# Filler matmuls in the waits of the first batch, another order of the first loads, later attentions, and loads held by semaphores, in a fused attention and FFN kernel

## Chip, cores, metric

One core of one Trainium2 chip. The metric is device time of the whole kernel in microseconds (us). The profile's span, from first to last instruction, is 1.7 to 3 us shorter than it, mostly 1.8. All runs here were of the fast state; ratios are the mean time of one kernel's fast runs over that of the other's of the same rounds, so not quite the ratio of the medians that are quoted beside them.

## The reference

Eight batches, 12 heads, 448 tokens, head size 64; then a gated FFN over all 3584 tokens.

```python
scores = np.matmul(q, k.transpose(0, 1, 3, 2)) / sqrt(64)
attn = np.maximum(scores, 0.0) ** 2 / 448
x = np.matmul(attn, v)            # (8, 12, 448, 64), then to (3584, 768)
g = x @ w_gate                    # 768 -> 1536
gelu = 0.5 * g * (1.0 + erf(g / sqrt(2)))
out = (gelu * (x @ w_val)) @ w_out
```

## The kernel before

The program is laid out ahead of time. Each piece of work is an `Op` with an assumed cost and with dependencies; `run_plan` goes through the queues in order of planned time and emits instructions in that order. The plan decides only the **order on each engine**; at run time semaphores alone hold anything. A dependency in the plan that isn't a data dependency holds nothing on the chip.

```python
# loads: queued on GpSimd, float32 in DRAM to bfloat16 in SBUF
def load(nbytes, emit, deps=(), cost=0.7):
    op = Op("POOL", cost, emit, deps)           # deps: for the plan only
    arrivals[op] = nbytes / 400e3
    POOL.append(op)
    return op
...
# order of the first loads
for h0, h1 in ((0, 2), (2, 4), (4, 8), (8, 12)):
    load_heads(0, h0, h1)                       # q, k, v of batch 0
load_w12(0)                                     # gate and value weights, 1 of 6
load_heads(1, 0, 4)
load_w12(1)
load_w12(2)
load_heads(1, 4, 8)
load_w12(3)
load_heads(1, 8, 12)
load_w12(4)
load_w12(5)
load_qk(2, 0, 0, H)
load_qk(2, 1, 0, H)
for i in range(FC // WOG):
    load_wo(i)                                  # output weights, 4 pieces
load_v(2, 0, H)
...
# q and k of batches 2 to 7 are turned by DMA: DVE copies into qkr, SyncE issues
copies = [Op("DVE", 0.4, lambda c=c: emit_copy(c), ...) for c in range(SC)]
tr_op[b] = [Op("SP", 1.1, lambda c=c: nc.sync.dma_start_transpose(...), ...) for c in range(SC)]
...
# where each batch's attention stands among the matmuls of the FFN
LEAD = 6.0
for b in range(B):
    if b == 0:
        lo, hi = -60.0, -12.0
    elif b == 1:
        lo, hi = -8.0, starts[1] - LEAD
    else:
        lo, hi = starts[b - 1] - LEAD, starts[b] - LEAD
```

In the profile PE is TensorE, ACT ScalarE, DVE VectorE, POOL GpSimd and SP SyncE (SPq: its DMA issues). `sp` are scores (PE), `rl` their ReLU (ACT), `attnT` its square (DVE), `ff` the PSUM tiles of everything else, `gel` the gelu (ACT), `uT` the gated product (DVE). TensorE is used as four 64x64 quarters.

## Time and profile before

| | before |
|---|---|
| time, median | 458.32 us (457.1 to 458.66) |
| span of the profiled run | 456.6 us |
| PE busy | 93% |
| mean granted clock | 0.950 |
| first gate matmul | 37.44 us |
| first gelu of batch 2 | 158.90 us |

The page, the windows, the waits and the chain are shown and read in the prediction. One line more, of the timeline of SyncE (start, length, what). It is the issue of batch 2's seven transposes:

```profile
61.85 26.17 SPq L248 DMA_TRANSPOSE qkT<-qkr  x7
```

### The profile page before, as it was taken

What the parts mean: (1) busy time and instruction counts of PE and PEld (TensorE: products, weight loads), DVE (VectorE), ACT (ScalarE), POOL (GpSimd) and SP (SyncE); (2) the same over time, 40 slices, a digit from 0 to 9 for tenths busy, and PEclk for the clock granted to TensorE, in tenths of its full rate; (3) what the DMA queues carried; (4) which work ended last, traced back from release to release, by engine and by line L of the source; (5) the groups of instructions that cost most, each with busy time, mean ns of one, the idle gap of its engine ahead of it and who ended that gap; (6) DMA issues with size and microseconds to landing.
All of it is one profiled execution on the core that took longest, in us unless ns stands there. A gap on an engine that the chain in (4) does not pass through costs nothing.

```text
span 456.6 us, 19815 instructions
## 1 busy us (share of the span) xinstructions
PE 423.8 (93%) x9192; PEld 366.7 (80%) x9192; DVE 206.0 (45%) x367; ACT 225.4 (49%) x322; POOL 70.7 (15%) x114
## 2 busy tenths in 40 slices
PE   5779997099999999999999999999999999999994
PEld 2546874078779987899999978899999878987894
DVE  1795574034574356634573357435653455212200
ACT  1786544035555655555555555555555655422221
POOL 9545421006000510033000600030000000000000
PEclk8597999579999999999999999999999999999997
DMA  7999999909455690749082873581272200120033
GB/s 99 191 198 198 201 199 168 191 3 182 83 79 82 109 190 7 121 87 200 15 118 60 141 143 38 88 137 41 15 112 73 72 3 3 37 72 3 3 83 93
DMA packets 75218, 44.92 MB, mean 98 GB/s; under 512 B 36224, under 2 KB 71552, under 8 KB 75136
## 3 DMA queue, kind: packets, MB, share of 16 engines
q0 software_dynamic: 37056, 24.39, 37.4%
q1 hardware_dynamic: 38080, 19.28, 22.2%
q8 instruction: 72, 1.18, 1.1%
q14 instruction: 10, 0.08, 0.0%
HBM read 48.76 MB, written 11.01 MB: 131 GB/s over the span
## 4 chain that ended last, share of the span: by engine, by line
PE 88%; DMA 3%; ACT 2%; POOL 2%; SPq 2%; DVE 2%; issue 1%; POOLq 0%; ACTq 0%; DVEq 0%
PE ff L151 79%; PE sp L151 8%; ACT rl L340 2%; SPq L248 2%; DMA qk<-in_k_dram 2%; DMA qkT<-qkr 1%; POOL qk L198 1%; POOL v L211 1%; PE ff L291 1%; DVE attnT L346 1%; DVE qkT L297 1%; DVE uT L438 0%; DVE xT L395 0%; ACT gel L433 0%; ACT osb L484 0%
## 5 line engine op out<-in xcount | busy, mean ns | idle before, releaser
L151 PE MATMUL ff<-xT,wv 64*64 64x448 bf16 x2304 | 223.4, 351 | 0.4 <-issue 0.4
L151 PE MATMUL ff<-xT,wg 64*64 64x448 bf16 x2304 | 222.4, 351 | 0.4 <-ACT gel L433 0.4
L340 ACT ACTIVATE rl<-sp 128x896 bf16<-128x896 f32 x168 | 152.4, 918 | 135.0 <-PE sp L151 105.4
L151 PE MATMUL ff<-wo,uT 64*64 64x384 bf16 x2688 | 151.1, 324 | 0.3 <-DVE uT L438 0.3
L151 PEld LDWEIGHTS <-wv 64*64 64x64 bf16 x2304 | 134.4, 107 | 15.7 <-issue 1.5
L151 PEld LDWEIGHTS <-wg 64*64 64x64 bf16 x2304 | 132.6, 107 | 15.9 <-issue 0.9
L346 DVE TENSOR_TENSOR attnT<-rl 128x896 bf16<-128x896 bf16 x168 | 104.0, 623 | 84.5 <-ACT rl L340 83.4
L151 PE MATMUL sp<-qkT 64*64 64x448 bf16 (+1 forms) x768 | 113.0, 349 | 20.6 <-DMA qkT<-qkr 14.2
L151 PEld LDWEIGHTS <-uT 64*64 64x64 bf16 x2688 | 127.1, 107 | 5.5 <-DVE uT L438 1.0
L438 DVE TENSOR_TENSOR uT<-gel,ff 128x448 bf16<-128x448 bf16 x96 | 59.5, 620 | 78.5 <-PE ff L151 75.6
L151 PE MATMUL ff<-attnT,v 64*64 64x448 bf16 (+1 forms) x768 | 91.5, 340 | 0.0
L433 ACT ACTIVATE gel<-ff 128x448 bf16<-128x448 f32 x96 | 52.1, 543 | 54.0 <-PE ff L151 51.6
L151 PEld LDWEIGHTS <-qkT 64*64 64x64 bf16 x768 | 47.7, 111 | 32.1 <-issue 26.2
L211 POOL DMA_DIRECT2D v<-in_v_dram x46 | 28.8, 651 | 197.4 <-PE ff L151 166.1
L151 PEld LDWEIGHTS <-v 64*64 64x64 bf16 x768 | 49.5, 111 | 3.5 <-issue 0.5
L395 DVE TENSOR_SCALAR xT<-ff 128x448 bf16<-128x448 f32 x48 | 29.9, 623 | 49.0 <-PE ff L151 46.8
L484 ACT COPY osb<-ff 128x384 f32<-128x384 f32 x56 | 26.7, 476 | 36.2 <-PE ff L151 36.2
L291 PEld LDWEIGHTS <-qk 64*64 64x64 bf16 x336 | 11.8, 136 | 7.8 <-DMA qk<-in_q_dram 3.1
L198 POOL DMA_DIRECT2D qk<-in_k_dram x23 | 14.7, 641 | 15.6 <-DMA wo<-in_moe_w_out_dram 8.6
L291 PE MATMUL ff<-ident,qk 64*64 64x64 bf16 x336 | 13.0, 221 | 4.2 <-DMA qk<-in_q_dram 2.9
L198 POOL DMA_DIRECT2D qk<-in_q_dram x23 | 14.9, 673 | 9.9 <-PE ff L151 6.3
L240 DVE COPY qkr<-qk 128x768 bf16<-128x768 bf16 x42 | 13.4, 356 | 0.0
(17 smaller groups left out, 30.2 us busy)
## 6 DMA issues: line engine op xcount, KB each, us to landing
out_dram<-osb SPq DMA_DIRECT2D x56, 192.0 KB, 2.7
v<-in_v_dram POOLq DMA_DIRECT2D x40, 128.0 KB, 5.6
qk<-in_q_dram POOLq DMA_DIRECT2D x20, 224.0 KB, 9.2
qk<-in_k_dram POOLq DMA_DIRECT2D x20, 224.0 KB, 9.8
wg<-in_moe_w_gate_dram POOLq DMA_DIRECT2D x6, 384.0 KB, 10.7
wv<-in_moe_w_val_dram POOLq DMA_DIRECT2D x6, 384.0 KB, 11.8
wo<-in_moe_w_out_dram POOLq DMA_DIRECT2D x4, 576.0 KB, 21.4
v<-in_v_dram POOLq DMA_DIRECT2D x2, 384.0 KB, 26.0
```

The source lines that it names most:

```text
L151: return nc.tensor.matmul(o, lhsT, rhs, start=start, stop=stop, tile_position=(P * row, P * col))
L198: op = load(4 * (h1 - h0) * S * D, lambda: nc.gpsimd.dma_start(tile_of().rearrange("p (h x) -> p h x", h=H)[:, h0:h1, :], src[b, h0:h1].re ...
L211: nc.gpsimd.dma_start(v16[b][HALF[i], h0:h1, :, :], v[b, h0:h1].rearrange("h (p c) d -> p h c d", c=SC)[:, :, c0:c0 + VC, :])
L240: nc.vector.tensor_copy(box[0][:, c], qk16[b].rearrange("p (h c d) -> p c h d", c=SC, d=D)[:, c])
L248: tr_op[b] = [Op("SP", 1.1, lambda c=c: nc.sync.dma_start_transpose(qkT_tile(b).rearrange("d (c r) x -> d c r x", c=SC)[:, c], box[0][:, c ...
L291: nc.tensor.transpose(t[HALF[j], pr, c * P:(c + 1) * P], src[HALF[i], 2 * (2 * m + pr) + j, c, :], ident[HALF[i], HALF[i]], tile_position= ...
L340: nc.scalar.activation(rl[:, :, :], box[0][:, :, 0:S], AF.Relu)
L346: nc.vector.tensor_tensor(a[:, :, :], box[1][:, :, :], box[1][:, :, :], op=ALU.mult)
L395: nc.vector.tensor_scalar_mul(xT[b][:, pr, :], box[0][:, 0:S], scalar1=out_scale)
L433: nc.scalar.activation(gel[b, fc][:, :], box[0][:, 0:S], AF.Gelu)
L438: nc.vector.tensor_tensor(uT[b][:, fc, :], gel.pop((b, fc))[:, :], box[0][:, 0:S], op=ALU.mult)
L484: nc.scalar.copy(ob[:, cols], box[0][:, 0:OGS])
```

## The change

Its intent: get PE through the start of the kernel sooner. (1) Where the plan leaves PE idle in the first 45 us, matmuls without a use are put in to keep its clock up. (2) The first loads come in larger pieces, weights before batch 1, output weights before q and k of batch 2. (3) Attention of batches 1 and 2 stands later among the FFN's matmuls. (4) Loads from batch 3 on get semaphores, so that what was only planned now holds; batch 3's are tied to later gates by three.

```diff
@@ run_plan: gaps of PE are offered to fill @@
         if e in together:
             floor = t
+            if t > busy:
+                fill(busy, t)
+            busy = max(busy, op.end)
@@ loads @@
     def load(nbytes, emit, deps=(), cost=0.7):
-        op = Op("POOL", cost, emit, deps)
+        def paced():
+            ins = emit()
+            for d in deps:
+                tc.add_manual_dep(ins.ins, d.ins.name, SYNC, reason="pace")
+
+        op = Op("POOL", cost, paced, deps)
@@ fillers (new; FILL = 45.0; new_bank also records the reader of each PSUM bank) @@
+    def fill(t0, t1):
+
+        n = int((t1 - t0 - 0.35) / 0.11)
+        if t1 > FILL or n < 2:
+            return
+        reader = in_bank[-FB] if len(in_bank) >= FB else None
+        if reader is not None and (reader.end is None or reader.end + 0.1 > t0):
+            return
+        t = new_bank(None)
+        for _ in range(n):
+            nc.tensor.matmul(t[:, 0:256], warm[:, 0:128], warm[:, 0:256], start=True, stop=True)
@@ add_gate_value: which gate releases which load @@
-            if b + 2 < B and b and fc < 9:
-                h0 = 4 * (fc % 3)
+            n = fc - (3 if b == 1 else 0)
+            if b + 2 < B and b and 0 <= n < 9:
+                h0 = 4 * (n % 3)
   ... (fc becomes n in the lines that follow)
@@ order of the first loads @@
-    for h0, h1 in ((0, 2), (2, 4), (4, 8), (8, 12)):
-        load_heads(0, h0, h1)
+    for h0, h1 in ((0, 4), (4, 8), (8, 12)):
+        load_qk(0, 0, h0, h1)
+        load_qk(0, 1, h0, h1)
+        if h0:
+            load_v(0, h0 - 4, h1 - 4)
+    load_v(0, 8, 12)
     load_w12(0)
+    load_w12(1)
     load_heads(1, 0, 4)
-    load_w12(1)
     load_w12(2)
+    load_w12(3)
     load_heads(1, 4, 8)
-    load_w12(3)
-    load_heads(1, 8, 12)
     load_w12(4)
     load_w12(5)
+    load_heads(1, 8, 12)
+    for i in range(FC // WOG):
+        load_wo(i)
     load_qk(2, 0, 0, H)
     load_qk(2, 1, 0, H)
-    for i in range(FC // WOG):
-        load_wo(i)
     load_v(2, 0, H)
@@ places of the attentions @@
-            lo, hi = -8.0, starts[1] - LEAD
+            lo, hi = 0.0, starts[1] - LEAD
+        elif b == 2:
+            lo, hi = starts[1] + 6.0, starts[2] - LEAD
```

Cut: the other uses of `new_bank`, `return` ahead of some `dma_start`, and the line that keeps the instruction of `uT` for the semaphore.

More of the change, by code (lines that the diff above doesn't have):

```diff
@@ L20, in __init__, with run_plan @@
         self.start = self.end = None
-def run_plan(queues, pools, arrivals, together):
+def run_plan(queues, pools, arrivals, together, fill):
     free = {e: 0.0 for e in (*queues, *pools)}
     at = {e: 0 for e in queues}
-    dma = last = floor = 0.0
+    dma = last = floor = busy = 0.0
     def ready(op):
@@ L119 @@
     FB = 4
+    FILL = 45.0
     EARLY = 2
@@ L178, in emit @@
         def emit(wt, src):
-            nc.gpsimd.dma_start(
+            return nc.gpsimd.dma_start(
                 wt[:, :, :], src[:, cols].rearrange("(c p) f -> p c f", p=128))
@@ L210, in emit @@
                 c0 = i * (SC - VC)
-                nc.gpsimd.dma_start(
+                return nc.gpsimd.dma_start(
                     v16[b][HALF[i], h0:h1, :, :],
@@ L258, with new_bank @@
     ring = [warm_op]
+    in_bank = []
+    def new_bank(reader, shape=(128, 512), dtype=f32):
+        in_bank.append(reader)
+        return psF.tile(list(shape), dtype, name="ff", tag="F")
+    def fill(t0, t1):
[8 more added lines that the diff above has]
+            nc.tensor.matmul(t[:, 0:256], warm[:, 0:128], warm[:, 0:256], start=True, stop=True)
     def ring_dep():
@@ L286, in emit @@
             if i not in box:
-                box[i] = psF.tile([128, 2, SC * P], bf16, name="ff", tag="F")
+                box[i] = new_bank(t_op[b, m, i], [128, 2, SC * P], bf16)
             t = box[i]
@@ L377, in emit @@
             if not box:
-                box[0] = psF.tile([128, 512], f32, name="ff", tag="F")
+                box[0] = new_bank(x_op[b, pr])
             if i == 1 and w == VC - 1:
@@ L422, in emit @@
             if not box:
-                box[0] = psF.tile([128, 512], f32, name="ff", tag="F")
+                box[0] = new_bank(done)
             if r == 1 and dc == 0:
@@ L437, in emit_mult @@
                 uT[b] = upool.tile([128, FC, S], bf16, name="uT", tag="uT")
-            nc.vector.tensor_tensor(uT[b][:, fc, :], gel.pop((b, fc))[:, :],
-                                    box[0][:, 0:S], op=ALU.mult)
+            u_op[b, fc].ins = nc.vector.tensor_tensor(
+                uT[b][:, fc, :], gel.pop((b, fc))[:, :], box[0][:, 0:S], op=ALU.mult).ins
         ops = [[Op(f"PE{r}", GS, lambda r=r, dc=dc: emit(r, dc),
@@ L450, in add_gate_value @@
             DVE.append(done)
-            if b + 2 < B and b and fc < 9:
-                h0 = 4 * (fc % 3)
-                if fc < 6:
-                    load_qk(b + 2, fc // 3, h0, h0 + 4, [done])
+            n = fc - (3 if b == 1 else 0)
+            if b + 2 < B and b and 0 <= n < 9:
+                h0 = 4 * (n % 3)
+                if n < 6:
+                    load_qk(b + 2, n // 3, h0, h0 + 4, [done])
                 else:
                     load_v(b + 2, h0, h0 + 4, [done])
-                if fc == 5:
+                if n == 5:
                     add_dma_transposes(b + 2)
@@ L469, in emit @@
             if not box:
-                box[0] = psF.tile([128, 512], f32, name="ff", tag="F")
+                box[0] = new_bank(cp)
             i, o = divmod(fc, WOG)
@@ L598, in emit_warm_up @@
     def emit_warm_up():
-        t = psF.tile([128, 512], f32, name="ff", tag="F")
+        t = new_bank(None)
         for _ in range(10):
@@ L606 @@
     run_plan({"PE0": PE0, "POOL": POOL}, {"PE1": PE1, "ACT": ACT, "DVE": DVE, "SP": SP, "IDLE": IDLE}, arrivals,
-             ("PE0", "PE1"))
+             ("PE0", "PE1"), fill)
 _INS = ['q', 'k', 'v', 'moe_w_gate', 'moe_w_val', 'moe_w_out']
```

## The prediction

> **What bounds the kernel now.** I read the page first, for the shape of the whole.
>
> ```profile
> PE   5779997099999999999999999999999999999994
> PEclk8597999579999999999999999999999999999997
> DMA  7999999909455690749082873581272200120033
> GB/s 99 191 198 198 201 199 168 191 3 182 83 79 82 109 190 7 121 87 200 15 118 60 141 143 38 88 137 41 15 112 73 72 3 3 37 72 3 3 83 93
> ```
>
> One slice is 11.4 us. From slice 10 on TensorE is full and at full clock: nothing to gain there but matmuls. The loss is in the first 100 us: clock at about half in slice 2, a hole in slice 8. DMA is flat at 191 to 201 GB/s from slice 2 to 6. Second view, the windows of that stretch (columns: length, then busy us of PE, weight loads, DVE, ACT, POOL, each with its count; clock, DMA share, GB/s).
>
> ```profile
> 0.00:10.00 10.00, 5.45 (x76) 2.84 (x76) 1.21 (x3) 1.28 (x1) 9.05 (x20) 0.90 0.73 89
> 10.00:20.00 10.00, 7.10 (x136) 4.38 (x140) 5.95 (x11) 7.12 (x9) 7.23 (x11) 0.50 1.32 185
> 20.00:30.00 10.00, 8.74 (x152) 6.01 (x154) 8.78 (x16) 8.91 (x12) 4.95 (x7) 0.75 1.41 198
> 30.00:40.00 10.00, 7.79 (x146) 5.17 (x141) 6.65 (x12) 6.20 (x8) 4.96 (x7) 0.76 1.41 198
> ...
> 80.00:90.00 10.00, 0.00 (x0) 0.00 (x0) 0.00 (x0) 0.00 (x0) 0.00 (x0) 0.50 1.26 191
> ```
>
> From 20 to 30 us ACT and DVE are near 90%: the first attention is bound by them, while PE is slow or waiting. From 80 to 90 us only DMA works. Third, the waits, and the chain through the hole (start, length, what).
>
> ```profile
> PE sp L151 <- DMA qkT<-qkr: 14.2, 1, 14.2
> ```
>
> ```profile
> 77.57 1.41 SPq L248
> 78.97 0.04 issue
> 79.02 6.17 SPq L248
> 85.22 6.42 DMA qkT<-qkr
> 91.64 0.14 issue
> 91.78 0.58 PE sp L151 x2
> ```
>
> The first scores of batch 2 (counted from 0) wait 14.2 us for its q and k, transposed by DMA. Fourth, the DMA view of two windows: batch 2's seven transposes (first line) against batch 3's (second).
>
> ```profile
> qkT<-qkr SPq DMA_TRANSPOSE x7, 13.5
> ```
>
> ```profile
> qkT<-qkr SPq DMA_TRANSPOSE x7, 2.8
> ```
>
> 13.5 us to landing against 2.8. The timeline of SyncE gives 26.17 us for issuing the first seven (from 61.85) and 10.32 for the others (from 128.88). In the first case batch 3's six q and k loads, issued by GpSimd between 61 and 75 us, share the engines.
>
> **What the Trainium skill says.** (1) "DMA: Bandwidth & Descriptors", section "Issuing engines are not separate DMA queues": transfers started by different engines run on the same 16 DMA engines and interleave. The 13.5 against 2.8 us agrees. (2) "TensorE: Matmul & The Clock Gate", Part 1: the array's clock is halved unless the recent window, some 3.4 us, was busy; an idle window brings it back to half. The trace agrees: 0.50 from 7 us, after a gap of 2.95, and 0.50 through the hole and until 97 us, 5 us after it. It also shows 0.50 between 35 and 43 us without a gap that long. (3) Same page, "Architectural detail": ACT and DVE take their instructions strictly in order, so one that waits for a load holds those behind it. The trace before doesn't show that decisively: its first copy into `qkr` starts at 61.25, and q and k landed at 61.0.
>
> **My ruler.** Four 64x64 matmuls of 448 columns share the array and cost 0.19 us (in the trace, successive pairs of the value matmuls start at 44.37, 44.56, 44.75, with gate pairs between). I walked through both compiled instruction orders and summed columns at that rate; "position" is that sum, in us of full-clock PE work. The whole is 396.4 before and 399.9 after. From the first gate of batch 2 (position 114.4, its gelu at 158.9 us) to PE's end at 450.9, 282.0 of position took 292.0 us: 1.035 us per unit of position. From that gate on the two orders of work are the same but for details, so I give the rest its measured length: 456.6 - 158.9 = **297.7 us**. What must be found is when the changed kernel reaches that gelu.
>
> **The change, part by part.**
>
> *Filler matmuls.* The order holds 32 more matmuls of 256 columns, in ten groups of 2 to 5, all before the first gate of batch 0: 3.4 us at full clock, in places where PE was planned to wait for ACT or DVE. Cost on the path 0 to 1 us. Their use is the clock: at half clock in the first attention 12 relus took 13.4 us (10.95 to 24.33), at full clock nine took 7.39. Worth 3 to 4 us of that stage, if they work.
>
> *Order of the first loads.* q and k of four heads first, v one group later; 18 issues become 12 for batch 0. GpSimd takes about 0.6 us per issue (1.21 us for two v of 64 KB), and before issued some 145 KB/us between 4 and 10 us, less than the 198 GB/s that DMA can do: so 89 GB/s in the first window. With larger pieces I expect full rate from about 4 us: 2.5 to 3 us earlier for everything behind.
>
> *Weights before batch 1, output weights before batch 2's q and k; second attention later.* The first gate (37.44 us before) had six score units of batch 1 before it, now one. Attention 0 starts near 8 instead of 10.95 and takes 18 to 21 us; q and k of batch 1's first heads land near 26; so the first gate is near 29.5, at position 19.6 (before: 17.0). But it isn't free to run from there. Landing times: bytes ahead over 0.1985 MB/us, plus an offset. Before, q, k of batch 2 had 10,176 KB up to and with them and landed at 61.0 (issue 45.30 + 15.7). Now they have the 2,304 KB of output weights ahead too: 12,480 KB, so 61.0 + 2.36 MB/0.205 (the rate at 50 to 60 us) = 72.5, less 2.5 to 3 for the earlier start: **69.5**.
>
> *A held DVE.* The first `qkr` copy of batch 2 stands in DVE's order before the last product into `uT` of batch 0. PE needs that one at position 56. PE itself gets there so: 29.5, plus 6.8 of position x 1.035 = 36.6 at batch 1's second transposes, whose q and k land near 38.2; then 29.6 x 1.035 = 30.6 to 68.9. The load is at 69.5 and four short DVE steps (2.3 us) follow: PE passes position 56 at **71.8**. So a wait of some 3 us, and a new bound: the loads.
>
> *Batch 3's loads held.* They now wait for DVE's products at positions from 74 on, some 91 us. Batch 2's transposes then share DMA only with v of batch 2 (0.79 MB, 4 us). Issue from 70.5 in some 10.3 us, plus 2 for sharing, plus 2.8: ready near 85.5. Their scores are at position 69.8 instead of 51.9: PE is there at 71.8 + 13.8 x 1.035 = 86.1. The 14.2 us wait and the 2.75 us lost to 5.5 us at half clock behind it go; I leave 1 us for a remainder.
>
> *Sum.* The gelu is at position 117.8: 71.8 + 61.8 x 1.035 + 1 = 136.8. Plus 297.7 = 434.5 of span. The time was 458.33 for the profiled run with 456.6 of span: add 1.7. **436 us**, 4.9% less.
>
> **The rivals.** (a) *The wait is replaced.* The hole was hidden DMA work; with 0.59 MB less of batch 3 in the way, but batch 2's q and k 11.5 us later in the queue, the transposes land late again, or PE stays half-clocked after the 3 us wait. For it: the queue is full until some 74 us in both orders. Against: scores moved by 17.9 of position. If 5 us of wait and 2.5 of cold clock remain: 443. (b) *Nothing of the start is gained*: DMA is bound by small pieces and not by GpSimd's issue rate, and filler does nothing. For it: 165 to 185 GB/s even at 10 to 16 us. Then q and k land at 72.5: 439. (c) *PE's own path is slower than I sum*, by cold clock in the first attention and fillers waiting for banks: gate 0 at 34 gives position 56 at 74: 438. (d) *Loads are faster* than my offset says: 69.5 becomes 67, PE's path binds: 433.
>
> **Range and chances.** The fixed 297.7 us is 65% of the time and hardly uncertain; all doubt lies in 136.8. The rivals cover 433 to 443; two together, or a stall I haven't seen, reach 446; all luck gives 429. Range 429 to 446. A result within 2% needs over 449.4, that is 13 us of new waits: 4%. Slower: 1%.
>
> **What would show it.** In the changed profile: first gate near 29.5 us; clock near full from 8 to 30; q and k of batch 2 landing near 69.5; a DVE wait of 0 to 4 us for them before a `qkr` copy, with PE idle some 3 us near 70; the seven transposes issued in 10 to 13 us; PE's wait for `qkT` under 3 us; batch 2's first gelu near 137; from there 298 us. The prediction is wrong if the wait for `qkT` is again above 6 us, if the clock falls to half for long after 30 us, or if the part behind that gelu isn't within 2 us of 297.7.

## The result, and the profile after

| | before | after |
|---|---|---|
| time, median | 458.32 us | 436.5 us (436.01 to 436.95) |
| ratio, 95% interval | | 0.9528 (0.9507 to 0.9549) |
| span of the profiled run | 456.6 us | 434.6 us |
| mean granted clock | 0.950 | 0.992 |
| first gate matmul | 37.44 us | 30.84 us |
| first gelu of batch 2 | 158.90 us | 137.60 us |
| from there to the end of the span | 297.7 us | 297.0 us |

21.3 of the 22.0 us of span were gained ahead of batch 2's first gelu. The page of the changed kernel, the rows that answer to those of before (slices of 10.9 us now):

```profile
PE   6999989999989999999999999999999999999995
PEclk9899999999999999999999999999999999999998
DMA  8999999826993679256933679357962100120034
GB/s 117 196 198 198 203 209 186 161 39 74 123 174 75 88 88 159 77 85 93 161 70 93 89 89 175 76 81 87 148 94 76 40 3 2 49 66 3 3 84 101
```

The hole is gone, and from slice 3 on the clock is at nine tenths or more. DMA still moves 196 to 209 GB/s from slice 2 to 6: the load queue is as full as before. The windows (same columns as in the prediction):

```profile
0.00:10.00 10.00, 6.48 (x89) 3.22 (x89) 2.15 (x4) 3.01 (x3) 7.51 (x17) 1.00 0.82 111
10.00:20.00 10.00, 9.14 (x208) 6.00 (x208) 7.66 (x14) 8.01 (x10) 7.21 (x10) 0.83 1.40 196
20.00:30.00 10.00, 9.16 (x171) 5.47 (x168) 9.21 (x18) 7.81 (x10) 4.93 (x7) 1.00 1.41 197
30.00:40.00 10.00, 9.83 (x205) 7.32 (x207) 5.38 (x10) 7.17 (x9) 4.50 (x6) 1.00 1.41 198
...
80.00:90.00 10.00, 10.00 (x215) 7.86 (x210) 2.65 (x5) 4.25 (x7) 0.00 (x0) 1.00 0.59 117
```

DMA moved 111 instead of 89 GB/s in the first 10 us: that's the new order and sizes, for every run with the old ones has 88 to 91 there, every run with the new ones 102 to 119. PE works through 80 to 90 us. The chain of the changed kernel through the place that had the hole:

```profile
51.04 19.61 DMA qk<-in_k_dram
...
70.73 0.36 DVE qkr L249
...
71.55 0.62 DVE qkr L249 x2
72.17 0.54 DVE uT L465
...
72.75 13.32 PE ff L155 x280
86.07 0.18 PE sp L155 x2
```

One reads it upwards: batch 2's scores at 86.07 follow 13 us of uninterrupted matmuls, those follow a product of DVE, that stands behind three copies into `qkr`, and those waited for k of batch 2, which landed 19.6 us after its issue. No wait stands between 72.75 and the scores: the last transpose had landed at 83.11.

This is one profile, though, and PE waited only 0.6 us for that product. In the profile of the same kernel run again (c_after, span 433.9 us) k landed at 70.77, and the chain passes the place on PE alone:

```profile
69.89 1.32 PE ff L155 x28
71.22 0.01 PE sp L155 x2
71.23 15.17 PE ff L155 x321
86.40 0.18 PE sp L155 x2
```

Here PE's own path and the load arrive within about a microsecond of each other. Of the six profiles that have holds, new places and new load order together (fillers in or out, batch 3's loads sooner or not), batch 2's load is in the chain of the first one only; the other five pass here by PE. The issue of the transposes, from SyncE's timeline of the changed kernel:

```profile
71.19 10.39 SPq L257 DMA_TRANSPOSE qkT<-qkr  x7
```

10.39 us instead of 26.17. The waits (total, times, longest, in us), those that matter of the first 110 us, and then PE's one wait for transposes in a wider window:

```profile
DVE qkr L249 <- DMA qk<-in_k_dram: 1.3, 1, 1.3
...
PE ff L155 <- DVE uT L465: 0.6, 1, 0.6
```

```profile
PE sp L155 <- DMA qkT<-qkr: 1.7, 1, 1.7
```

This 1.7 us isn't batch 2 but **batch 3**, whose last transposes landed at 126.28. Batch 3's loads, held three gates longer, made its own transposes late, which the prediction had not seen. (In c_after's profile they landed at 125.62, and PE stood 0.7 us at that place.)

### The profile page after: what moved, and what is told of

It reads as the page before. It is cut to its first block, busy times and chain, and to the rows that moved or that the text cites. A ratio compares the mean times of both kernels' runs of the same rounds, so it can differ in the third digit from the quotient of the medians.

```text
span 434.6 us, 19901 instructions
## 1 busy us (share of the span) xinstructions
PE 420.1 (97%) x9224; PEld 365.5 (84%) x9224; DVE 205.7 (47%) x367; ACT 225.5 (52%) x322; POOL 68.4 (16%) x110
## 3 DMA queue, kind: packets, MB, share of 16 engines
q0 software_dynamic: 36992, 24.39, 42.2%
HBM read 48.76 MB, written 11.01 MB: 138 GB/s over the span
## 4 chain that ended last, share of the span: by engine, by line
PE 86%; DMA 7%; ACT 2%; DVE 1%; issue 1%; POOL 1%; POOLq 0%; ACTq 0%; DVEq 0%
PE ff L155 78%; PE sp L155 7%; DMA qk<-in_k_dram 6%; ACT rl L367 2%; DMA qkT<-qkr 1%; PE ff L318 1%; DVE attnT L373 1%; POOL qk L207 1%; PE ff L285 1%; DVE uT L465 0%; DVE qkr L249 0%; DVE qkT L324 0%; ACT osb L512 0%; POOL ident masks.py:199 0%; POOL ident masks.py:197 0%
## 5 line engine op out<-in xcount | busy, mean ns | idle before, releaser
L155 PE MATMUL ff<-xT,wg 64*64 64x448 bf16 x2304 | 218.2, 349 | 0.2 <-issue 0.2
L155 PE MATMUL ff<-xT,wv 64*64 64x448 bf16 x2304 | 218.0, 349 | 0.0
L155 PEld LDWEIGHTS <-wg 64*64 64x64 bf16 x2304 | 130.6, 107 | 14.9 <-issue 0.8
L155 PEld LDWEIGHTS <-wv 64*64 64x64 bf16 x2304 | 130.4, 107 | 13.6 <-issue 1.0
L155 PE MATMUL sp<-qkT 64*64 64x448 bf16 (+1 forms) x768 | 107.9, 331 | 3.6 <-DMA qkT<-qkr 1.7
L465 DVE TENSOR_TENSOR uT<-gel,ff 128x448 bf16<-128x448 bf16 x96 | 59.5, 620 | 79.3 <-PE ff L155 71.2
L155 PE MATMUL ff<-attnT,v 64*64 64x448 bf16 (+1 forms) x768 | 86.2, 326 | 0.0
L155 PEld LDWEIGHTS <-qkT 64*64 64x64 bf16 x768 | 45.5, 107 | 13.8 <-issue 8.6
L155 PEld LDWEIGHTS <-v 64*64 64x64 bf16 x768 | 47.0, 107 | 3.5 <-issue 0.2
L318 PEld LDWEIGHTS <-qk 64*64 64x64 bf16 x336 | 8.9, 116 | 6.5 <-DMA qk<-in_k_dram 4.2
L249 DVE COPY qkr<-qk 128x768 bf16<-128x768 bf16 x42 | 13.6, 363 | 1.3 <-DMA qk<-in_k_dram 1.3
L318 PE MATMUL ff<-ident,qk 64*64 64x64 bf16 x336 | 10.4, 200 | 3.8 <-DMA qk<-in_k_dram 2.7
```

The costliest lines, as they stand in the source:

```text
L155: return nc.tensor.matmul(o, lhsT, rhs, start=start, stop=stop, tile_position=(P * row, P * col))
L249: nc.vector.tensor_copy(box[0][:, c], qk16[b].rearrange("p (h c d) -> p c h d", c=SC, d=D)[:, c])
L318: nc.tensor.transpose(t[HALF[j], pr, c * P:(c + 1) * P], src[HALF[i], 2 * (2 * m + pr) + j, c, :], ident[HALF[i], HALF[i]], tile_position= ...
L465: u_op[b, fc].ins = nc.vector.tensor_tensor(uT[b][:, fc, :], gel.pop((b, fc))[:, :], box[0][:, 0:S], op=ALU.mult).ins
```

## The experiments

Twelve runs in three groups, each against the kernel before on the same chip. By my check, with all parts taken out of the changed kernel the instructions of all engines were again those of the kernel before. The diff too leaves only bookkeeping besides the parts named here.

| run | what | median us | ratio to before (95%) |
|---|---|---|---|
| the change | | 436.5 | 0.9528 (0.9507 to 0.9549) |
| a_nohold | changed, holds out | 456.84 | 0.9964 (0.9937 to 0.9991) |
| a_oldplace | changed, old places | 449.21 | 0.9816 (0.9781 to 0.9851) |
| a_oldloads | changed, old order of loads | 442.75 | 0.967 (0.9634 to 0.9705) |
| a_nofill | changed, fillers out | 438.2 | 0.9551 (0.9524 to 0.9578) |
| b_hold | before, holds in | 453.67 | 0.9895 (0.9874 to 0.9917) |
| b_place | before, new places | 455.94 | 0.9943 (0.9923 to 0.9964) |
| b_loads | before, new order of loads | 452.82 | 0.9878 (0.9851 to 0.9906) |
| a_noshift | changed, batch 3's loads three gates sooner | 436.95 | 0.9529 (0.9485 to 0.9573) |
| c_after | the change again | 436.55 | 0.9525 (0.9503 to 0.9548) |
| c_nofill | fillers out again | 439.12 | 0.96 (0.9566 to 0.9633) |
| c_vfirst | changed, v of batch 2 ahead of q, k | 439.94 | 0.9606 (0.9582 to 0.963) |
| c_nofill_noshift | fillers out, loads sooner | 436.71 | 0.9524 (0.9499 to 0.9548) |

**Theory L:** the changed kernel's end is set by when q and k of batch 2 land; the holds keep their transposes quick; all behind batch 2's first gelu is fixed. **Rival P:** PE's own path from the first gate on sets the end. **Rival S:** it is the later place of the scores that counts, not the holds.

### Holds out (a_nohold)

```diff
         def paced():
             ins = emit()
-            for d in deps:
-                tc.add_manual_dep(ins.ins, d.ins.name, SYNC, reason="pace")
```

> The changed kernel without the semaphores that hold the loads from batch 3 on; the plan and the order of instructions are kept. Theory C (the loads of batch 3 slowed the transposes of batch 2): they are issued from about 60 us, right behind v of batch 2, the issue of the seven transposes takes 18 to 26 us instead of 10.4, and the scores of batch 2 wait 5 to 10 us for qkT near 86: 441 to 448 us. Rival S (it is enough that the scores stand later in PE's order): no wait there, and batch 3's 1.7 us wait for its transposes goes: 434.5 to 437.

Measured 456.84 us: almost the whole gain is gone, more than either side had said. SyncE's timeline, and PE's wait:

```profile
71.25 26.08 SPq L255 DMA_TRANSPOSE qkT<-qkr  x7
```

```profile
PE sp L155 <- DMA qkT<-qkr: 15.9, 1, 15.9
```

The transposes start at the same 71.2 us and take 26.08 us again. Why the expectation (a wait of 5 to 10 us) was too low is in GpSimd's timeline of this run:

```profile
70.97 0.61 POOL L205 DMA_DIRECT2D qk<-in_k_dram  x1 [2.74 <-DMA qk<-in_k_dram]
78.93 0.61 POOL L218 DMA_DIRECT2D v<-in_v_dram  x1 [7.35 <-PE ff L155]
79.70 2.44 POOL L218 DMA_DIRECT2D v<-in_v_dram  x4 [0.17 <-issue]
...
83.87 0.61 POOL L205 DMA_DIRECT2D qk<-in_q_dram  x1 [0.94 <-DMA qk<-in_k_dram]
...
91.70 1.23 POOL L205 DMA_DIRECT2D qk<-in_k_dram  x2
```

I had counted only batch 3's q and k. But in the new order batch 1's attention is done, so v of batch 3 and then q and k of **batch 4** find free buffers and follow at once, in the middle of batch 2's transposes. Rival S falls: without the holds the later scores, with all other parts in, save 1.5 us.

### Holds alone on the kernel before (b_hold)

The parts of load order, places and fillers are taken out of the changed kernel; the holds and the shift by three stay.

> The kernel before with one part of the change alone: loads from batch 3 on held by semaphores (and batch 3's moved three gates later). Theory C (batch 3's q and k loads are what made batch 2's transposes late): with their 1.38 MB gone from 61 to 90 us, the transposes share DMA only with output weights and v until about 74, and are ready near 80 to 83 instead of 91.6; PE waits 3 to 6 us instead of 14.2: 446 to 450 us. Rival (the output weights and v of batch 2 were enough to delay them): 455 to 458.

Measured 453.67 us, 4.9 us less, outside both expectations.

```profile
61.89 20.60 SPq L257 DMA_TRANSPOSE qkT<-qkr  x7
```

```profile
PE sp L155 <- DMA qkT<-qkr: 6.6, 1, 6.6
```

With batch 3's loads gone the issue still takes 20.60 us, while the output weights land until 73.9 and v of batch 2 until 81.0 us. The wait is halved, 6.6 instead of 14.2 us. So the cause that I gave for the hole before, batch 3's loads, is about half of it. By elimination the other half is left to what was queued right behind q and k of batch 2, the output weights and v; a_oldloads, below, has that order too, with holds and places in, and its issue takes 21.98 us. Of the 7.6 us, 2.0 are given back to a new wait for batch 3's transposes.

### Old places (a_oldplace)

```diff
-            lo, hi = 0.0, starts[1] - LEAD
-        elif b == 2:
-            lo, hi = starts[1] + 6.0, starts[2] - LEAD
+            lo, hi = -8.0, starts[1] - LEAD
```

> The changed kernel with the old places of the attentions of batch 1 (from -8) and batch 2 (from 6 us ahead of batch 1's gates): batch 2's scores stand at position 58.3 instead of 69.8. Theory: transposes are ready near 85.5 as before, so PE waits for them with 11.5 units of work less done: 446 to 452 us, with a wait for qkT of 4 to 10 us. Rival (place matters little once batch 3's loads are held): 436 to 440.

Measured 449.21 us, as the theory had it. The transposes are as quick as in the changed kernel (issued from 71.47 in 9.91 us), but PE stands at their scores sooner, with less done:

```profile
PE sp L155 <- DMA qkT<-qkr: 4.2, 1, 4.2
PE ff L318 <- DMA qk<-in_k_dram: 4.1, 3, 2.1
```

The longest of the second line is the other attention: batch 1's first piece, moved forward again, waits 2.1 us for its k until 27.8 us (the other two are batch 0's), and the first gate comes at 35.54 us. Batch 3's transposes, later, cost PE another 2.4 us, which the expectation didn't have.

### New places alone on the kernel before (b_place)

> The kernel before with the new places of the attentions alone. Batch 2's scores stand at position 60.6 instead of 51.9. Theory: batch 3's loads aren't held, transposes are ready near 91.6 again, PE waits for them with 8.7 units more done: 9 us gained, 447 to 451 us, the wait still 4 to 9 us. Rival (the wait vanishes since scores come after the last load): 440 to 445.

Measured 455.94 us, 2.6 us less where I had expected 9. The expectation kept the transposes ready at 91.6; they were not:

```profile
63.24 27.44 SPq L255 DMA_TRANSPOSE qkT<-qkr  x7
```

The issue takes 27.44 us, about as before, and the last transpose lands at 98.99 instead of 91.64. Beside the last of them now stand v of batch 3 (issued from 83.83) and q and k of batch 4 (from 91.22), as in the run without holds. PE waits 13.6 us. A better place gave its gain back through the load queue.

### Old order of loads (a_oldloads)

```diff
-    for i in range(FC // WOG):
-        load_wo(i)
     load_qk(2, 0, 0, H)
     load_qk(2, 1, 0, H)
+    for i in range(FC // WOG):
+        load_wo(i)
     load_v(2, 0, H)
```

and the first lines of it as in the kernel before (two heads at a time).

> The changed kernel with the old order and sizes of the first loads. Theory L: everything starts 2.5 to 3 us later, q and k of batch 2 no longer hold PE (they land near 61), but the output weights, now last, need the same bytes ahead and land near 74: 438 to 441 us. Rival P (only the place of the attentions, the fillers and the holds matter): 435.5 to 437.5. Rival W (weights later than batch 1 starve the gates): above 444.

Measured 442.75 us, past the upper end of theory L. Its chain:

```profile
51.73 24.09 DMA wo<-in_moe_w_out_dram
...
75.86 5.50 PE ff L155 x117
...
81.38 0.64 DVE xT L422
82.02 1.40 SPq L257
...
83.46 2.82 DMA qkT<-qkr
...
86.42 0.38 PE sp L155 x2
```

The mechanism is as the theory had it, output weights landing last (75.8, I had said 74), and what I left out is visible two lines on: the transposes, now issued beside those weights, took 21.98 us and PE waited 2.2 us for them. The first gate came at 33.84 instead of 30.84 us. Rival P as this expectation words it, that the order of loads doesn't matter, falls.

### New order of loads alone (b_loads)

> The kernel before with the new order and sizes of the first loads alone. Theory: a part that hurts by itself. It starts 2.5 to 3 us earlier, but q and k of batch 2 land near 70 instead of 61 with their scores at position 54, and batch 3's loads share DMA with the transposes: ready near 95 or later, PE waits 10 to 20 us: 456 to 466 us. Rival (an earlier start is worth its 3 us): 452 to 455.5.

Measured 452.82 us: faster, so the theory that this part hurts alone was wrong, and its rival right in the number.

```profile
71.96 15.74 SPq L255 DMA_TRANSPOSE qkT<-qkr  x7
```

q and k of batch 2 did come late (transposes from 71.96 instead of 61.85), but with the output weights already in, only v of batch 2 and batch 3's q and k are beside them: 15.74 us instead of 26.17. The last lands at 89.2 instead of 91.6, and PE waits 10.2 instead of 14.2 us.

### Fillers out (a_nofill, c_nofill)

```diff
-    FILL = 45.0
+    FILL = 0.0
```

> The changed kernel without its 32 filler matmuls, all else kept. Theory L (the end is set by q and k of batch 2, which land near 70.6 us, and PE gets to position 56 of its work at about the same time): the clock falls to half in the first attention, the first gate comes 2 to 4 us after 30.8, part of it is hidden behind the loads: 437.5 to 439.5 us. Rival P (PE's own path from the first gate on sets the end, the loads have nothing to do with it): the whole delay is seen, 439.5 to 442. Rival N (fillers do nothing but cost time): 433 to 436.

> The changed kernel without fillers once more, in more rounds: in the first run it was at 438.2 us in a range of 436.1 to 438.4. Theory F (fillers are worth what their clock is worth, 1 to 2 us): 437.5 to 438.5, and over the unaltered kernel by more than the interval. Rival N (they do nothing that can be measured): within 0.5 us of it.

The first time 438.2 us with an interval that overlaps the changed kernel's; the second time 439.12 against 436.55 in the same rounds, intervals apart. Over all runs: eight with fillers at 435.7 to 437.0, mean 436.4; ten without at 436.1 to 442.8, mean 438.7. So fillers look worth some 2.3 us here. Two things speak against taking that as settled: with batch 3's loads sooner (below) the mean is 436.9 with fillers and 436.3 without, and the delay that I expected, a first gate 2 to 4 us later, isn't in the profiles: 30.52 and 32.33 us without fillers, 30.84 and 31.71 with them. Is it the clock? The mean granted clock of those runs is 0.9915 with fillers and 0.9856 without; 0.0059 of 435 us is 2.6 us, about the difference. But one profile doesn't show it. The 10 to 20 us windows of c_after first, then of c_nofill (busy time of PE, PEld, DVE, ACT and POOL with counts, then the granted clock):

```profile
10.00:20.00 10.00, 9.59 (x176) 5.76 (x172) 7.34 (x13) 8.96 (x11) 7.41 (x11) 0.69 1.40 196
```

```profile
10.00:20.00 10.00, 8.95 (x161) 6.16 (x157) 7.05 (x13) 8.55 (x10) 6.58 (x10) 1.00 1.40 196
```

In c_nofill's profiled run the clock in that window was 1.00 without any filler, in c_vfirst's it was 0.50 with all of them. Fillers don't fix the clock. That they act through it fits the means and isn't shown by a run that isolates it.

### q and k of batch 2 later by one load (c_vfirst, with c_after as yardstick)

```diff
+    load_v(2, 0, H)
     load_qk(2, 0, 0, H)
     load_qk(2, 1, 0, H)
-    load_v(2, 0, H)
```

> The changed kernel once more, unaltered, as the yardstick on the chip of the three runs that follow: 436 to 437 us, ratio to before 0.951 to 0.955.

> The changed kernel with v of batch 2 loaded ahead of its q and k, which then land some 3.9 us later (0.79 MB at 0.2 MB/us), near 74.5. Theory L (the arrival of q and k of batch 2 is on the path that sets the end): the transposes are ready near 89 instead of 85 and PE, at their scores near 86, waits 2 to 4 us: 438 to 440.5 us. Rival P (PE's own path is the later one and has room): 436 to 437.

Measured 439.94 us against 436.55: 3.4 us more, inside the range of theory L. But the edit did more than delay a load. The plan also put all seven copies into `qkr` behind the last product into `uT` of batch 0 in DVE's order, so that they no longer hold it, and two output stores among the transposes on SyncE:

```profile
76.73 4.11 SPq L257 DMA_TRANSPOSE qkT<-qkr  x3
80.89 1.23 SPq L517 DMA_DIRECT2D out_dram<-osb  x2
82.16 5.97 SPq L257 DMA_TRANSPOSE qkT<-qkr  x4
```

Its chain near the scores, and PE's wait there:

```profile
73.78 13.15 PE ff L155 x275
86.92 3.79 DMA qkT<-qkr
...
90.75 0.38 PE sp L155 x4
```

```profile
PE sp L155 <- DMA qkT<-qkr: 1.5, 1, 1.5
```

Against c_after, k landed at 75.36 instead of 70.77 (4.6 us later) and the last transpose at 90.71 instead of 83.19 (7.5 us later). In c_after that was 3.2 us before PE came to the scores, so this room was used up first, and PE then waited 1.5 us. PE was late on its own, too: the first gate came at 34.10 instead of 31.71, after a first attention with the clock at 0.50 from 10 to 20 us (c_after: 0.69), and batch 1's last transposes on PE at 58.33 instead of 56.06. These 2.3 us, from before the place in question, are about half of the 4.3 us between the two profiled spans.

So the run shows that q and k lengthen the kernel when they come so late that the room is gone. It doesn't show that their arrival sets the end of the change as it stands: theory L isn't shown, and c_after's chain fits rival P. That 3.4 us lie near the 3.9 us of the delay is chance, as far as the record shows.

### Batch 3's loads sooner (a_noshift, c_nofill_noshift)

```diff
-            n = fc - (3 if b == 1 else 0)
+            n = fc
```

> The changed kernel with batch 3's held loads issued from the first gate of batch 1 on instead of the fourth. In the changed kernel PE waits 1.7 us for batch 3's transposes. Theory: that wait goes, and the loads, from about 84 us on, come after the transposes of batch 2 (issued 71.2 to 81.6): 434.5 to 436 us. Rival (they meet the end of batch 2's transposes and delay its scores): 436.5 to 439.

> A candidate for a better kernel: no fillers, and batch 3's held loads from the first gate of batch 1 on. If fillers do nothing (N) and the 1.7 us wait for batch 3's transposes goes: 434.5 to 436 us. If fillers are worth 1 to 2 us (F): 436 to 437.5.

In both profiles the wait for batch 3's transposes is gone, as expected. The time isn't better: 436.95 (434.7 to 438.9) with fillers (on another chip), 436.71 without, against 436.55. Without fillers it looks worth 2.4 us (439.12 to 436.71), with them nothing. The spread of single runs, 2 to 4 us, is as large as what is looked for; this stays open, and no version was found that clearly beats the change.

## Why the prediction was right

**Shape and fixed part: right.** The part behind batch 2's first gelu is 297.0 us against 297.7 (296.8 to 298.3 in the profiles of all runs), and the rest reached that gelu at 137.6 against 136.8.

**Loads: the arrival right, 1.1 us optimistic; that it sets the end isn't shown.** q and k of batch 2 landed at 70.6 against 69.5. They are in the chain of one profile in six. A reading under it was wrong: GpSimd's 145 KB/us between 4 and 10 us holds until 6.4 us only. From 6.42 to 8.84 it issued 704 KB, some 290 KB/us, while DMA moved 136 GB/s (6.3 to 8.7 us), so there the issue rate wasn't the limit, as rival (b) had it. Of the 2.5 to 3 us that I expected from the earlier start, 1.9 came.

**The held DVE: the wait is there, 1.3 us; PE's idle time isn't.** I had PE at that product at 68.9, waiting some 3 us; it came at 72.15 and waited 0.6 (in c_after not at all). PE's own path came later than my sum: first gate at 30.84 instead of 29.5, with the clock at 0.83 instead of near full between 10 and 20 us, and from there 41.3 instead of 39.4 us. That is rival (c), in part. The sum took the later of two arrivals, and the one that I had put 3 us earlier came out level with it: that the product was done at 72.7 against 71.8 is partly luck.

**Transposes: right in the changed kernel, half right in cause.** Issue 10.39 us as predicted without the 2 us for sharing, the last landing at 83.11 against 85.5, PE at the scores at 86.07 against 86.1. But in naming batch 3's q and k as what made them slow before, I named half: b_hold shows 20.60 us of issue without those. In the changed kernel the output weights are in before, so the other half is removed by the load order, not by the holds (21.98 us of issue with the holds and the old order). And the holds keep off more than I counted: v of batch 3, q and k of batch 4 (a_nohold).

**The term that I booked for the wrong thing.** I left 1 us for a remainder at batch 2; that was zero, and 1.7 us were lost at batch 3 instead (0.7 in c_after's profile).

**Fillers: overrated as a clock guard.** "Clock near full from 8 to 30" doesn't hold in every run. In the mean some 2.3 us, not settled; I had 3 to 4 in their stage. Two readings of the clock before were loose: it fell at 7.91 us, inside the gap of 5.49 to 8.44 and not after it, and behind the hole it was at half for 4.9 us (91.78 to 96.66), not 5.5.

**The parts don't add up.** Alone on the kernel before, holds, places and load order give 4.9, 2.6 and 5.7 us, 13 together; taken out of the changed kernel they cost 20.3, 12.7 and 6.2. Holds and load order take loads away from beside the same transposes, the places give PE other work meanwhile; with any one missing PE waits at the scores again, 15.9, 4.2 and 2.2 us. The Trainium skill, "DMA: Bandwidth & Descriptors", section "SWDGE vs HWDGE vs iDMA", says that loads from GpSimd and transposes from SyncE feed different internal queues of the same engines, served in turn. That fits 10.4 us with little beside them and 15.7 to 27.4 with loads queued; no run here shows the turns themselves.

## What to carry to other kernels

A plan orders an engine's instructions but holds nothing on the chip: a load queue runs as far ahead as buffers let it, so each improvement that frees buffers sooner also lets more loads in front of something urgent, unless a semaphore says otherwise. When several transfers make one thing late, the parts of a cure look small one at a time; judge each by taking it out of the whole as well as by adding it alone. And before saying which arrival sets the end, profile the same kernel twice: here two paths arrive together, and the chain follows now one, now the other. A delay put in on purpose is a test only if it delays nothing else and the room in front of it is known; in c_vfirst 3.4 us for 3.9 looked like proof and wasn't.

## What the Trainium skill lacked or had wrong

- "DMA: Bandwidth & Descriptors", section "Rules for kernel authors", says that a transpose next to ordinary DMAs needs nothing. That is about correctness; the cost is missing. Here seven transposes of 128x768 bfloat16 took 10.4 us to issue with only v of batch 2 beside the first of them, and 15.7 to 27.4 us with more loads queued.
- Same page, section "Where 436 GB/s comes from", has the HBM side, some 358 GB/s, bind for loads. The loads here read float32 and write bfloat16: 198 GB/s written from 20 to 50 us, and the page of the profile has 48.76 MB read from HBM for 24.39 MB that this queue moved, so some 396 GB/s read (an estimate), with one core at work. The measured table of the same page, which says that the other core was idle, goes above 358 too; that section's sentence lacks the condition.
- "TensorE: Matmul & The Clock Gate", Part 1, ties the half clock to idle windows and names frequent short idles as a second way to it, but not how busy PE must be in a window. Before, the clock was at half from 35.2 to 42.0 us though no gap there was longer than 0.83 us; in the window of 10 to 20 us the same program (the change and its repeat) had 0.83 and 0.69.
- No page says what fillers are worth: here 32 matmuls of 256 columns gave some 2.3 us in the mean of 8 and 10 runs, nothing in another pair of kernels, and the clock was still at half in parts of some runs.
